# Streaming an MLP's first weights by rows instead of from re-laid column blocks

## The chip, the cores and the metric

The kernel runs on one core of one Trainium2 chip. The time is the device time of one execution in microseconds (us); a run list is quoted by its median. A profile is one execution of the kernel recorded by the hardware.

## The reference, cut to what matters

Two layers alternate twice: an attention layer (A) with recurrent memory over 64 segments of 32 tokens, and a Mixer layer (B) over the same 2048 tokens of width 640. The change touches B alone.

```python
def _B_ref(x, w1, w2, w3, w4):            # w1, w2: 640x640; w3: 640x1536; w4: 1536x640
    h = _gelu(_layernorm(x, axis=-1) @ w1)
    c = D // 4                            # 160 columns a group
    g0 = jnp.pad(h[:, :, 0*c:1*c], ((0,0),(1,0),(0,0)))[:, :S, :]     # one token later
    g1 = jnp.pad(h[:, :, 1*c:2*c], ((0,0),(0,1),(0,0)))[:, 1:, :]     # one earlier
    g2 = ...   # two later
    g3 = ...   # two earlier
    hs = jnp.concatenate([g0, g1, g2, g3], axis=-1) @ w2
    x1 = x + hs
    h2 = _gelu(_layernorm(x1, axis=-1) @ w3) @ w4
    return x1 + h2
...
x = x + A(layernorm(x)); x = x + B(layernorm(x))     # and both once more
```

## The kernel before

Both A layers run as two lanes, 40 columns of a matmul each, one segment per step; the second lane follows 5 steps behind. So there are 69 steps of about 50 us. Every two steps a chunk of Mixer (64 tokens of each lane, so 128 columns) runs among the attention: 35 chunks. A planner written in Python, before anything runs, places each operation on its engine. It takes what can start first by its own estimates, and among operations that could start nearly at the same time the one with the earlier `due`. The programs of the engines then wait for each other by semaphores.

Most of the weights stream from DRAM through a ring of 16 buffers in SBUF, on-chip memory (tile `wst`). Attention may hold 14 of them and Mixer 6. Attention's are issued by SyncE, Mixer's by GpSimd. Of the banks of PSUM, the memory that matmuls sum into, the kernel keeps two for the sums of `psy` and `y`, and shares six: class P (projections psq, psk, psv) may hold 4, class S (scores and the like: pss, pst, pso, psvt) 3, Mixer's class B 2.

```python
RING = 16; RING_A = 14; RING_B = 6
STEP = 48.0
W3 = (0.7, 0.04)        # due of w3's loads: from 0.7 of a step, every 0.04
PSUM_BANKS = {"y": 2, "x": 6}
PSUM_USES = {"y": ("y", 2), "P": ("x", 4), "S": ("x", 3), "B": ("x", 2)}
...
# Plan.place(): per engine e
lim = m + (LOOK if e == "PE" else 0.05)        # m: the earliest possible start
s, o = min((so for so in vals if so[0] <= lim), key=lambda so: (so[1].due, so[1].i))
```

w1's columns were taken in an order that puts each group's first 128 columns in one block and all the groups' remaining 4 x 32 in the fifth. The columns of w3 were taken in 12 blocks of 128. To make such a block one plain transfer, the kernel first copied w1, w3 and the last block of w2 within DRAM (`wbd`), in its first 25 us:

```python
def load_b(c, nm, n, due):
    b = ring("rb")
    k = {"w1": n, "w3": KC + n, "w2": KC + FC - 4 + n}.get(nm)
    ...
        src, rd = wbd[k], [B("wbd", k)]
    # nc.gpsimd.dma_start(out=T(b)[:, 0:Dm], in_=src)

def order_mixer_weights():
    for n in range(KC):             # five blocks of w1, gathered columns
        ...
    ...                             # one of w2
    for n in range(FC):             # twelve of w3
        def f3(op, n=n):
            o = wbd[KC + n].rearrange("p (kc n) -> p kc n", kc=KC)
            nc.gpsimd.dma_start(out=o, in_=B_w3.rearrange("(kc p) n -> p kc n", p=P)[:, :, P*n:P*n + P])
```

A column block completes 128 outputs by itself. Three of them share a PSUM bank, which goes to gelu while the next bank fills:

```python
for i, (a, e) in enumerate(((0, 3), (3, KC))):          # w1: banks of 3 and 2 blocks
    pz = ps("B", [P, 3, XB], f32, "psh")
    for n in range(a, e):
        due = D(0.15 + 0.04 * n)
        wb, wv = load_b(c, "w1", n, due)
        def fw(op, n=n, a=a, wv=wv, pz=pz):
            w, o = wv(), T(pz)
            for kc in range(KC):
                nc.tensor.matmul(out=o[:, n - a, :], lhsT=w[:, kc*P:(kc+1)*P],
                                 rhs=vT[:, kc, 4:XB + 4], start=(kc == 0), stop=(kc == KC - 1))
        add("PE", mm_us(128, k=KC), due, fw, r=(wb, vTk, B("vTl")), a=(pz,))
    ...
    gelu(pz, e - a, i, due, outs, (B("hTB", i),))
# w2: five blocks, the shift in time is an offset into hTB (W2OFF) -> bank pair hs
# w3: four banks of three blocks each, same loop; then w4 in 12 blocks -> bank pair y
```

gelu is: ScalarE square, VectorE scale and multiply, ScalarE tanh, VectorE (1 + tanh) times the sum, written into `outs`.

## Time and profile before

| Quantity | Before | From |
|---|---|---|
| time, median of 3 runs | 3567.71 us | times |
| PE busy in the whole span | 95% | page |
| PE busy, 1000 to 2000 us | 97.9% | stretches |
| PE time not used by matmuls, 400 to 3200 us | 124 us | matmul starts, as in the prediction |
| psk and psq waiting for their streams, 130 to 3440 us | 34 us | waits of PE |
| last chunk of Mixer alone, from the last psy to the last y matmul | 42.0 us | timeline |

In a page, "PE" is the matmul side of TensorE and "PEld" its weight loads. A line of a stretch gives its bounds and length, busy us (and count) of PE, PEld, DVE (VectorE), ACT (ScalarE) and POOL (GpSimd), then the granted clock, the DMA engines' busy share and GB/s. A line of the waits reads: engine, tile and line of the waiter, "<-", what it waited for, then us in total, times, longest. The page leaves numbers out of names: `in_B_w_dram` is any of w1 to w4. The lines themselves stand in the prediction.

### The profile page before, as it was taken

To read this page: it belongs to the slowest core of one execution; us is meant where nothing else is said; L and a number is where in the kernel's file an instruction comes from. 1 tells how busy PE (TensorE), PEld (TensorE's weight loads), DVE (VectorE), ACT (ScalarE), POOL (GpSimd) and SP (SyncE) were. 2 spreads that over 40 slices of the span, in tenths; PEclk is the share of its full clock that TensorE was granted. 3 is DMA by queue.
4 is the path that set the end of the run, shared out by engine and by line. 5 is a ranking of instruction groups with operands and counts; after the bars stand their busy time and mean duration, and the time that the engine had idled before them with its cause. 6 is when DMAs were issued, how large, how long until landed. Compare 5 with 4: busy or idle time off the path is not lost.

```text
span 3573.5 us, 194593 instructions
## 1 busy us (share of the span) xinstructions
PE 3398.9 (95%) x84703; PEld 3260.5 (91%) x84703; DVE 2384.2 (67%) x7085; ACT 1710.5 (48%) x3584; POOL 948.2 (27%) x1712
## 2 busy tenths in 40 slices
PE   5899999999999999999999999999999999999996
PEld 4788999999999999999999999999999999999885
DVE  2456667777676777776666777776767777776555
ACT  2344555554454555544455555454545555444432
POOL 3022222222222222222222222222222222222224
PEclk9999999999999999999999999999999999999898
DMA  9999999999999999999999999999999999999996
GB/s 342 310 314 312 305 302 304 310 308 308 309 307 313 314 308 304 316 300 308 306 308 311 311 301 305 308 319 308 309 311 310 311 306 313 309 304 316 310 313 207
DMA packets 735993, 1097.76 MB, mean 307 GB/s; under 512 B 97374, under 2 KB 693612, under 8 KB 735136
## 3 DMA queue, kind: packets, MB, share of 16 engines
q1 hardware_dynamic: 669504, 874.19, 74.6%
q0 software_dynamic: 65632, 211.12, 17.9%
q8 instruction: 662, 10.85, 1.3%
q14 instruction: 195, 1.60, 0.1%
HBM read 1079.68 MB, written 8.19 MB: 304 GB/s over the span
## 4 chain that ended last, share of the span: by engine, by line
PE 69%; DMA 19%; issue 9%; POOL 2%; DVE 1%; ACT 0%; POOLq 0%; SPq 0%; ACTq 0%; DVEq 0%
PE psy L669 14%; PE psq L530 12%; PE psv L571 11%; PE psk L530 11%; DMA wst<-in_A_Wk_dram 7%; DMA wst<-in_A_Wq_dram 5%; PE psvt L583 4%; DMA wst<-in_B_w_dram 4%; PE pss L602 3%; PE pso L650 3%; PE psh L993 3%; DMA wst<-in_A_Wv_dram 3%; PE pst L635 2%; PE y L1011 2%; POOL wst L465 1%
## 5 line engine op out<-in xcount | busy, mean ns | idle before, releaser
L530 PEld LDWEIGHTS <-wst 128*128 128x128 bf16 x13248 | 551.9, 100 | 75.1 <-DMA wst<-in_A_Wk_dram 41.3
L587 ACT COPY V<-psvt 80x768 bf16<-80x768 bf16 (+1 forms) x552 | 438.2, 794 | 327.7 <-PE psvt L583 326.2
L465 POOL DMA_DIRECT2D wst<-in_B_w_dram x560 | 303.6, 542 | 1005.2 <-PE psk L530 250.6
L656 DVE CAST oT<-pso 128x480 bf16<-128x480 f32 (+1 forms) x552 | 340.8, 617 | 341.7 <-PE pso L650 341.0
L465 POOL DMA_DIRECT2D wst<-wbd x630 | 339.6, 539 | 724.8 <-PE pss L602 229.5
L669 PE MATMUL psy<-oT,wo 128*128 128x80 bf16 (+1 forms) x10350 | 509.6, 199 | 11.2 <-DMA wo<-in_A_Wo_dram 5.1
L538 ACT CAST qT<-psq 128x480 bf16<-128x480 f32 (+1 forms) x552 | 292.3, 530 | 428.8 <-PE psq L530 427.5
L530 PE MATMUL psk<-hT,wk 128*128 128x80 bf16 (+1 forms) x9936 | 482.7, 199 | 7.9 <-ACT hT L707 4.2
L571 PE MATMUL psv<-hT,wv 128*128 128x80 bf16 (+1 forms) x9936 | 466.6, 199 | 6.5 <-DMA wv<-in_A_Wv_dram 4.3
L530 PE MATMUL psq<-hT,wq 128*128 128x80 bf16 (+1 forms) x9936 | 454.5, 199 | 9.8 <-DMA wq<-in_A_Wq_dram 8.7
L577 ACT CAST vTs<-psv 128x480 bf16<-128x480 f32 (+1 forms) x552 | 292.3, 529 | 337.2 <-PE psv L571 335.5
L669 PEld LDWEIGHTS <-wo 128*128 128x128 bf16 x10350 | 425.6, 100 | 21.3 <-issue 9.2
L530 PEld LDWEIGHTS <-wk 128*128 128x128 bf16 x9936 | 411.6, 99 | 21.9 <-issue 8.8
L571 PEld LDWEIGHTS <-wv 128*128 128x128 bf16 x9936 | 399.8, 100 | 18.7 <-DMA wv<-in_A_Wv_dram 5.7
L613 DVE CUSTOM_DVE_ANT_1 pss<-pss,mask 80x320 f32<-80x320 f32 (+1 forms) x512 | 245.4, 479 | 253.8 <-PE pss L602 252.3
L530 PEld LDWEIGHTS <-wq 128*128 128x128 bf16 x9936 | 395.5, 100 | 16.3 <-DMA wq<-in_A_Wq_dram 9.5
L530 PE MATMUL psk<-hT,wst 128*128 128x80 bf16 (+1 forms) x6624 | 359.0, 199 | 32.2 <-DMA wst<-in_A_Wk_dram 28.2
L571 PE MATMUL psv<-hT,wst 128*128 128x80 bf16 (+1 forms) x6624 | 368.0, 199 | 8.7 <-DMA wst<-in_A_Wv_dram 4.8
L625 DVE TENSOR_REDUCE sm<-pss 80x4 f32<-80x320 f32 (+1 forms) x552 | 252.7, 458 | 153.6 <-ACT pss L620 153.1
L669 PE MATMUL psy<-oT,wst 128*128 128x80 bf16 (+1 forms) x6210 | 353.0, 199 | 1.0 <-DMA wst<-in_A_Wo_dram 0.5
L530 PE MATMUL psq<-hT,wst 128*128 128x80 bf16 (+1 forms) x6624 | 333.2, 200 | 16.3 <-DMA wst<-in_A_Wq_dram 14.3
L546 DVE CAST kT<-psk 128x320 bf16<-128x320 f32 (+1 forms) x552 | 254.7, 461 | 136.9 <-PE psk L530 132.6
(119 smaller groups left out, 5768.8 us busy)
## 6 DMA issues: line engine op xcount, KB each, us to landing
wst<-in_A_Wk_dram SPq DMA_DIRECT2D x1104, 192.0 KB, 4.7
wst<-in_A_Wq_dram SPq DMA_DIRECT2D x1104, 192.0 KB, 4.9
wst<-in_A_Wv_dram SPq DMA_DIRECT2D x1104, 192.0 KB, 4.9
wst<-in_A_Wo_dram SPq DMA_DIRECT2D x1242, 160.0 KB, 4.4
wst<-wbd POOLq DMA_DIRECT2D x630, 160.0 KB, 5.1
wst<-in_B_w_dram POOLq DMA_DIRECT2D x560, 160.0 KB, 4.9
wk<-in_A_Wk_dram SPq DMA_DIRECT2D x8, 576.0 KB, 7.3
wq<-in_A_Wq_dram SPq DMA_DIRECT2D x8, 576.0 KB, 7.5
```

The lines of the kernel that those rows point to most:

```text
L465: return (nc.sync if B_SP else nc.gpsimd).dma_start(out=T(b)[:, 0:Dm], in_=src)
L530: nc.tensor.matmul(out=o[:, c, 0:N], lhsT=w[:, c * P:(c + 1) * P], rhs=h[:, kc, c0:c0 + N], start=pq.begin(), stop=True, skip_group_check= ...
L538: nc.scalar.copy(out=q[:, :, 0:N], in_=T(pq)[:, :, 0:N])
L546: nc.vector.tensor_copy(out=k4[:, :, 0::3, 0:N], in_=p4[:, :, 0::2, 0:N])
L571: nc.tensor.matmul(out=o[:, c, 0:N], lhsT=w[:, c * P:(c + 1) * P], rhs=h[:, kc, c0:c0 + N], start=pv.begin(), stop=True, skip_group_check= ...
L577: nc.scalar.copy(out=vs[:, :, 0:N], in_=T(pv)[:, :, 0:N])
L583: nc.tensor.transpose(out=T(pt)[0:N, c, :], in_=vs[:, c, 0:N], identity=ident[:, :])
L587: nc.scalar.copy(out=V_[0:N, :, 0:Dh], in_=T(pt)[0:N].rearrange("n c f -> n (c f)").rearrange("n (i e) -> n i e", i=HG))
L613: nc.vector.tensor_tensor_reduce(out=o, in0=o, in1=maskt.unsqueeze(1).to_broadcast([N, HG, N]), scale=-scale, scalar=3.0e38, op0=ALU.add, ...
L625: nc.vector.reduce_sum(out=sm_[0:N, 4:4 + HG], in_=o, axis=AX.X)
L656: nc.vector.tensor_copy(out=o_[:, :, 0:N], in_=T(pso)[:, :, 0:N])
L669: nc.tensor.matmul(out=T(psy[j])[:, m - m0, c0:c0 + N], lhsT=w[:, m * P:(m + 1) * P], rhs=o_[:, c, 0:N], start=psy[j].begin(), stop=True, ...
```

## The change

The intent is to do without the copies. Rows of w1 and w3 are contiguous in DRAM as they lie. A block of 128 rows holds a part of the sum of every output, so all the outputs must stay open in PSUM until the last block: five column groups over two banks for w1, six over two banks for each half of w3. Without the gathered column order, w1's outputs lie in their plain order, and each 160-column group must be written shifted by gelu: nine pieces where there were six. Mixer's ring share goes from 6 to 5 and w3's loads are spaced wider.

```diff
-RING_B = 6
+RING_B = 5
-W3 = (0.7, 0.04)
+W3 = (0.75, 0.055)
+W1 = (0.15, 0.04)
...
-    wbd = dram.tile([KC + FC + 1, P, Dm], bf16, name="wbd")
...
     def load_b(c, nm, n, due):
         b = ring("rb")
-        k = {"w1": n, "w3": KC + n, "w2": KC + FC - 4 + n}.get(nm)
+        wd = Dm
+        if nm == "w1":
+            src = B_w1[P * n:P * n + P, :]
+        elif nm == "w3":
+            wd = F // 2
+            src = B_w3[P * (n % KC):P * (n % KC) + P, wd * (n // KC):wd * (n // KC) + wd]
...
-    def order_mixer_weights():        (whole function and its call)
...
-        for i, (a, e) in enumerate(((0, 3), (3, KC))):
-            pz = ps("B", [P, 3, XB], f32, "psh")
-            for n in range(a, e):
...
+        pz = [ps("B", [P, 3, XB], f32, "psh") for _ in range(2)]
+        for kc in range(KC):
+            due = D(W1[0] + W1[1] * kc)
+            wb, wv = load_b(c, "w1", kc, due)
+
+            def fw(op, kc=kc, wv=wv, pz=pz):
+                w = wv()
+                for n in range(KC):
+                    nc.tensor.matmul(out=T(pz[n // 3])[:, n % 3, :], lhsT=w[:, P * n:P * n + P],
+                                     rhs=vT[:, kc, 4:XB + 4], start=pz[n // 3].begin(), stop=True,
+                                     skip_group_check=True)
+            add("PE", mm_us(128, k=KC), due, fw, r=(wb, vTk, B("vTl")), a=tuple(pz))
...
+        outs = [], []
+        for n in range(KC):
+            p0 = 0
+            while p0 < P:
+                gi = (P * n + p0) // QD
+                p1 = min(P, QD * (gi + 1) - P * n, p0 + 32 if p0 % 64 else (P if p0 == 0 else p0 + 64))
+                o2 = 2 * (4 - W2OFF[gi])
+                outs[n // 3].append((p0, p1, n % 3, n % 3 + 1, hv[p0:p1, n:n + 1, o2:o2 + XB]))
+                p0 = p1
+        for i in range(2):
+            gelu(pz[i], 3 - i, i, due, outs[i], (B("hTB", i),))
...
-                off = W2OFF[n] if n < 4 else 0
-                lhsT = hTB[:, n, off:off + TOK, :].rearrange("p w l -> p (w l)")
+                lhsT = hTB[:, n, 0:TOK, :].rearrange("p w l -> p (w l)")
...
-        for i in range(4):             (w3, three column blocks to a bank)
...
+        for hf in range(2):
+            pz = [ps("B", [P, 3, XB], f32, "psh2") for _ in range(2)]
+            for kc in range(KC):
+                due = D(W3[0] + W3[1] * (KC * hf + kc))
+                wb, wv = load_b(c, "w3", KC * hf + kc, due)
+                ...                    (six matmuls a row block, over both banks)
+            for i in range(2):
+                a = 6 * hf + 3 * i
+                gelu(pz[i], 3, i, due, [(0, P, 0, 3, h2T[:, a:a + 3, :])], (B("h2T", 2 * hf + i),))
```

More of the change, by code (lines that the diff above doesn't have):

```diff
@@ L455, in load_b @@
         b = ring("rb")
-        k = {"w1": n, "w3": KC + n, "w2": KC + FC - 4 + n}.get(nm)
-        if nm == "w4":
-            src, rd = w4_v[:, n, :], []
-        elif nm == "w2" and n < 4:
-            src, rd = B_w2[QD * n:QD * n + P, :], []
+        wd = Dm
[4 more added lines that the diff above has]
+            src = B_w3[P * (n % KC):P * (n % KC) + P, wd * (n // KC):wd * (n // KC) + wd]
+        elif nm == "w4":
+            src = w4_v[:, n, :]
         else:
-            src, rd = wbd[k], [B("wbd", k)]
+            src = B_w2[P * n:P * n + P, :]
         def fn(op):
-            return (nc.sync if B_SP else nc.gpsimd).dma_start(out=T(b)[:, 0:Dm], in_=src)
-        add("SP" if B_SP else "POOL", SP_US if B_SP else POOL_US, due, fn, r=rd, w=(b,), dma=P * Dm * 2, queue="wb")
-        return b, lambda: T(b)[:, 0:Dm]
-    def order_mixer_weights():
-        for n in range(KC):
-            def f(op, n=n):
-                o = wbd[n].rearrange("p (kc n) -> p kc n", kc=KC)
-                w1 = B_w1.rearrange("(kc p) n -> p kc n", p=P)
-                if n < 4:
-                    nc.gpsimd.dma_start(out=o, in_=w1[:, :, QD * n:QD * n + P])
-                    return
-                for gi in range(4):
-                    nc.gpsimd.dma_start(out=o[:, :, 32 * gi:32 * gi + 32], in_=w1[:, :, QD * gi + P:QD * gi + QD])
-            add("POOL", 0.9 if n < 4 else 4.0, 20 + n, f, w=(B("wbd", n),), dma=P * Dm * 2)
-        def f2(op):
-            for gi in range(4):
-                nc.gpsimd.dma_start(out=wbd[KC + FC][32 * gi:32 * gi + 32, :], in_=B_w2[QD * gi + P:QD * gi + QD, :])
-        add("POOL", 4.0, 26, f2, w=(B("wbd", KC + FC),), dma=P * Dm * 2)
-        for n in range(FC):
-            def f3(op, n=n):
-                o = wbd[KC + n].rearrange("p (kc n) -> p kc n", kc=KC)
-                nc.gpsimd.dma_start(out=o, in_=B_w3.rearrange("(kc p) n -> p kc n", p=P)[:, :, P * n:P * n + P])
-            add("POOL", 0.9, 30 + n, f3, w=(B("wbd", KC + n),), dma=P * Dm * 2)
+            return (nc.sync if B_SP else nc.gpsimd).dma_start(out=T(b)[:, 0:wd], in_=src)
+        add("SP" if B_SP else "POOL", SP_US if B_SP else POOL_US, due, fn, w=(b,), dma=P * wd * 2, queue="wb")
+        return b, lambda: T(b)[:, 0:wd]
     def lanes(t):
@@ L929, in chunk @@
         add("POOL", 0.4, D(0.05), fhh, w=(B("hTB", 0), B("hTB", 1)))
-        for i, (a, e) in enumerate(((0, 3), (3, KC))):
-            pz = ps("B", [P, 3, XB], f32, "psh")
-            for n in range(a, e):
-                due = D(0.15 + 0.04 * n)
-                wb, wv = load_b(c, "w1", n, due)
-                def fw(op, n=n, a=a, wv=wv, pz=pz):
-                    w, o = wv(), T(pz)
-                    for kc in range(KC):
-                        nc.tensor.matmul(out=o[:, n - a, :], lhsT=w[:, kc * P:(kc + 1) * P],
-                                         rhs=vT[:, kc, 4:XB + 4], start=(kc == 0), stop=(kc == KC - 1))
-                add("PE", mm_us(128, k=KC), due, fw, r=(wb, vTk, B("vTl")), a=(pz,))
-            hv = hTB[:].rearrange("p k w l -> p k (w l)")
-            if e <= 4:
-                outs = [(0, P, 0, e - a, hv[:, a:e, 8:8 + XB])]
-            else:
-                outs = [(0, P, 0, 4 - a, hv[:, a:4, 8:8 + XB])]
-                for gi in range(4):
-                    o2 = 2 * (4 - W2OFF[gi])
-                    outs.append((32 * gi, 32 * gi + 32, 4 - a, 5 - a, hv[32 * gi:32 * gi + 32, 4:5, o2:o2 + XB]))
-            gelu(pz, e - a, i, due, outs, (B("hTB", i),))
@@ new lines, in chunk @@
+        hv = hTB[:].rearrange("p k w l -> p k (w l)")
+        outs = [], []
[9 more added lines that the diff above has]
+            gelu(pz[i], 3 - i, i, due, outs[i], (B("hTB", i),))
@@ L982, in chunk, with fw @@
         add("ACT", act_us(KC * XB), D(0.55), fe3, r=(ps3,), w=(vTk,))
-        for i in range(4):
-            a, e = 3 * i, 3 * i + 3
-            pz = ps("B", [P, 3, XB], f32, "psh2")
-            for n in range(a, e):
-                due = D(W3[0] + W3[1] * n)
-                wb, wv = load_b(c, "w3", n, due)
-                def fw(op, n=n, a=a, wv=wv, pz=pz):
-                    w, o = wv(), T(pz)
-                    for kc in range(KC):
-                        nc.tensor.matmul(out=o[:, n - a, :], lhsT=w[:, kc * P:(kc + 1) * P],
-                                         rhs=vT[:, kc, 0:XB], start=(kc == 0), stop=(kc == KC - 1))
-                add("PE", mm_us(128, k=KC), due, fw, r=(wb, vTk), a=(pz,))
-            gelu(pz, 3, i % 2, due, [(0, P, 0, 3, h2T[:, a:e, :])], (B("h2T", i),))
+        for hf in range(2):
[3 more added lines that the diff above has]
+                wb, wv = load_b(c, "w3", KC * hf + kc, due)
+                def fw(op, kc=kc, wv=wv, pz=pz):
+                    w = wv()
+                    for n in range(6):
+                        nc.tensor.matmul(out=T(pz[n // 3])[:, n % 3, :], lhsT=w[:, P * n:P * n + P], rhs=vT[:, kc, 0:XB],
+                                         start=pz[n // 3].begin(), stop=True, skip_group_check=True)
+                add("PE", mm_us(128, k=6), due, fw, r=(wb, vTk), a=tuple(pz))
+            for i in range(2):
+                a = 6 * hf + 3 * i
+                gelu(pz[i], 3, i, due, [(0, P, 0, 3, h2T[:, a:a + 3, :])], (B("h2T", 2 * hf + i),))
     def chunk_end(c):
@@ L1077, in start @@
             add("ACT", act_us(KC * SEG), -90 + s, f5, r=(p1,), w=(B("hT", s, "x0"),))
-        order_mixer_weights()
     start()
```

## The prediction

> **What bounds the kernel now.** I read four views in this order: the page's busy shares and slices, the busy time per stretch, the list of who waited for whom, and PE's timeline of the last 50 us.
>
> The page first (span; busy us, share and count of each engine; then the 40 slices):
>
> ```profile
> span 3573.5 us, 194593 instructions
> PE 3398.9 (95%) x84703; PEld 3260.5 (91%) x84703; DVE 2384.2 (67%) x7085; ACT 1710.5 (48%) x3584; POOL 948.2 (27%) x1712
> PE   5899999999999999999999999999999999999996
> ...
> DMA  9999999999999999999999999999999999999996
> ```
>
> PE and the DMA engines are both above nine tenths in every slice but the first two and the last. So there are three stages: a start, a long even middle, and a tail. The busy time per stretch (columns: stretch, its length, PE, PEld, DVE, ACT, POOL busy us with counts, granted clock, DMA share, GB/s) says what limits each:
>
> ```profile
> 10.00:20.00 10.00, 5.13 (x105) 4.33 (x105) 2.25 (x9) 2.11 (x8) 10.00 (x16) 1.00 1.07 376
> ...
> 80.00:100.00 20.00, 13.88 (x275) 11.11 (x273) 3.76 (x15) 3.94 (x9) 0.00 (x0) 1.00 1.07 366
> ...
> 1000.00:2000.00 1000.00, 978.97 (x24325) 954.67 (x24323) 703.82 (x2030) 504.47 (x1031) 263.59 (x474) 1.00 0.94 309
> ...
> 3500.00:3574.00 74.00, 42.10 (x709) 32.70 (x709) 33.66 (x94) 18.28 (x41) 34.60 (x63) 0.77 0.54 175
> ```
>
> In the start, until about 110 us, the DMA share stands at 1.07 and 366 to 376 GB/s while PE is busy half to two thirds: the start is bound by transfers. In the middle PE is 98% busy, and DMA runs at 0.94 and 309 GB/s, which is 83% of the 371 GB/s it showed it can do: the middle is bound by PE, with DMA close behind. The tail is a chain of latencies: the last Mixer chunk has no attention beside it.
>
> How much slack is left in the middle? From the trace's matmul starts between 400 and 3200 us I took the distance of each of 67,992 from the next, which sums to 2800 us, and subtracted the columns of each at 2.4 per ns plus 2.5 ns[...], which sums to 2676 us. Only 124 us are left to win there by any means. The waits of PE (middle only, 130 to 3440 us: waiter, what it waited for, us in total, times, longest) name the largest parts:
>
> ```profile
> PE psk L530 <- DMA wst<-in_A_Wk_dram: 22.7, 40, 1.4
> PE y L1011 <- DMA wst<-in_B_w_dram: 13.3, 25, 1.5
> PE psq L530 <- DMA wst<-in_A_Wq_dram: 11.2, 19, 1.4
> ```
>
> No line of the Mixer's w1 or w3 loads stands among the large ones: the loads of the copies (wst<-wbd) cost PE 0.8 us in the whole run. What PE waits for there is attention's streams and w4.
>
> **What the Trainium skill says.** (1) "DMA: Bandwidth & Descriptors", section "Issuing engines are not separate DMA queues": transfers issued from any engine run on the same 16 DMA engines. The trace agrees: while GpSimd issues the copies at 10 to 20 us, the total stays at 376 GB/s, no higher than the 371 to 372 later without them, so their bytes displace weights. (2) The same page, "Why small descriptors are slow (HBM only)": a 256-byte descriptor pays 27% bus overhead unless consecutive ones are put in one packet. The copies are cut into 256-byte and 64-byte pieces, so they could be dear, but the trace's packet records show them as packets of 4096, 2048 and 2560 bytes, and 4096 bytes took 178 ns (23 GB/s for an engine) against 73 ns for the 1536 bytes of attention's rows (21 GB/s): not dear here. (3) "TensorE: Matmul & The Clock Gate", "Back-to-back issue gap": 128 columns take N/2.4 + 2.5 = 56 ns. The trace agrees: ten psh matmuls at 3516.06 us span 0.72 us, and less the 0.22 us of the last that is 9 distances of 56 ns. (4) "PSUM — Partial Sum Buffer", "The four PSUM rules": a start flag clears the written marks of the whole bank, so several sums open in one bank need the flag on the first matmul alone. That is what the new loops do; so summing by rows over two banks needs no extra instruction. No run so far shows a cost of it.
>
> **The change, part by part.**
>
> *Copies removed.* The page says that 8.19 MB are written to DRAM: out 2.62, x2d 2.62, and 18 blocks of 163,840 bytes, 2.95 MB, the copies. Packets: 512 of 4096 B at 178 ns, 256 of 2048 B at 90, 158 of 2560 B at 107, 22 of 3840 B at 215: 91 + 23 + 17 + 5 = 136 us of one engine, 8.5 us of all 16. They are issued from 4.9 to 24 us, in the stage bound by transfers, so nearly all 8.5 us come off the path: **-8.5 us**. GpSimd also loses 24 issues (21 us busy), which hold back nothing before 115 us, where the first Mixer chunk starts.
>
> *Streaming w1 and w3 by rows.* w1: 5 blocks of 160 KB as before. w3: 10 blocks of 128x768 (192 KB) in place of 12 of 160 KB: the same 1.97 MB per chunk. So 32 loads per chunk in place of 34, 1120 in place of 1190. A contiguous block went as 5120-byte packets at 243 ns; half rows of w3 must go as 1536 bytes at 73 ns: 47.5 against 47.7 ns per KB, no difference. 70 issues fewer at 0.54 us each is 38 us of GpSimd, which is 27% busy: **0 us**.
>
> *Matmuls.* By the two builds' instruction orders both have 84,703, of the same shapes in the same numbers (2975 for w1 and w3). The order of attention's transfers on SyncE is the same line for line. Only the place of Mixer's matmuls among attention's moves: **0 us** of PE.
>
> *Shifts made by gelu.* The last gelu step of w1 was one 128x384 (543 ns), one 128x128 (276) and four 32x128 (282): 1.95 us per chunk. Now it is nine pieces of 128 columns at about 280: 2.5 us. 35 chunks x 0.57 = 20 us of VectorE, 67% busy: hidden in the middle.
>
> *Two banks held together.* w1 and each half of w3 now keep both Mixer banks from the first row to the end of the gelus; the two halves of w3 can't overlap. In the middle attention fills PE meanwhile. In the tail it shows:
>
> ```profile
> 3537.80 2.83 PE L939 MATMUL psh<-vT,wst 128*128 128x128 bf16 x25 [0.78 <-ACT vT L914]
> 3542.53 2.83 PE L961 MATMUL hs<-wst,hTB 128*128 128x320 bf16 x10 [1.90 <-issue]
> ...
> 3550.86 5.17 PE L993 MATMUL psh<-vT,wst 128*128 128x128 bf16 x60 [0.83 <-ACT vT L981]
> 3556.19 1.98 PE L1011 MATMUL y<-wst,h2T 128*128 128x320 bf16 x10 [0.16 <-DVE h2T L781]
> ```
>
> The first gelu of w1 began 1.1 us before psh x25 was over (3539.65, by the timeline of all engines); now it waits for all 25, and has 0.6 us more VectorE: about +1.5 us. For w3, a gelu takes 3.5 us (3552.65 to 3556.1); a half is 30 x 56 ns = 1.7 us, its two gelus end about 4.5 us later, and only then the other half starts: 2 x (1.7 + 4.5) = 12.4 us to the last h2T, after which three pairs of y matmuls take 0.8: y ends 13.2 us after the start of w3 against 11.7 now (3550.86 to 3562.58): **+3 us** for both.
>
> *Ring.* Mixer may hold 5 of the 16 ring buffers in place of 6, so attention gets one more at the busiest times, and w3's loads are due every 0.055 of a 48 us step (2.6 us) in place of 1.9: smoother. This should take some of the 34 us that psk and psq wait for their streams in the middle and could add to y's 13. I choose **-6 us**, a judgement.
>
> Sum: 3567.7 - 8.5 + 3 - 6 = 3556; I take **3555**.
>
> **Rivals.** *PSUM becomes the wait.* With both Mixer banks held, attention has 4 of the 6 shared banks for longer (about 1.6 steps in place of 1 in each pair of steps). For it: the scores and projections may ask for 7. Against: PE's unused time is no higher while hs or y hold two banks than elsewhere; binned over the chunk, it peaks at the step ends instead. If it happened, I'd expect 0.5 us per step, 35 us: 3590. *DMA is the true bound of the middle.* Then fewer buffers for Mixer and smoother loads would lift the whole 124 us by a good part: 3567.7 - 8.5 - 50 = 3510. Against it: 309 of 371 GB/s, and PE's waits on DMA there sum to 50 us. *The start is hidden anyway*: if PE had to wait for something else at 100 us, the 8.5 us vanish and the time stays at 3565. Against: PE's longest waits up to 130 us, after the first data, name wq, wo and wv arriving.
>
> **Range and chances.** The three runs before span 8 us. Start and tail together are worth -5, certain to about 5; the middle may go 25 us either way as the order on PE moves. 3530 to 3574 should hold it 8 times in 10. 2% is 71 us, more than half of all that PE leaves unused in the middle, so faster by 2% has 0.03, slower by 2% 0.03, and the same 0.94.
>
> **What would show it.** HBM written falls to 5.24 MB, read by 2.95 MB. The stretch in which the DMA share is above 1.05 ends some 8 us earlier. PE's busy share from 1000 to 2000 us stays within 97 to 99%. The waits of psk and psq on their streams fall, those of y may rise. In the tail psh for w3 comes as two groups of 30 with a gap of some 4 us. I'm wrong if the middle moves by over 25 us: then bank waits (psk or pss waiting for ACT or DVE) or stream waits must have changed by that much.

## More of the kernel before

In the compiled program an instruction waits only for the bank that it was given.

## The result and the profile after

The changed kernel took 3571.62 us (median of 4 runs, 3565.49 to 3574.00) and the kernel before 3565.85 us (4 runs, 3561.39 to 3569.81). The ratio is 1.0014, with a 95% interval of 0.9996 to 1.0032: the same. A ratio here is always the mean time of one kernel's fast runs over that of the other's of the same rounds, so it is not quite the ratio of the medians. The time is inside the predicted range and 17 us above the predicted value. The profiled executions were 3575.23 us (before) and 3571.54 us (changed).

The page of the changed kernel, its span, busy times and bytes:

```profile
span 3569.8 us, 194617 instructions
...
PE 3394.6 (95%) x84703; PEld 3260.5 (91%) x84703; DVE 2383.4 (67%) x7190; ACT 1709.6 (48%) x3584; POOL 895.0 (25%) x1618
...
HBM read 1076.73 MB, written 5.24 MB: 303 GB/s over the span
```

The same 84,703 matmuls take the same time. VectorE has 105 instructions more and isn't busier. GpSimd has 94 fewer. The written bytes have fallen from 8.19 to 5.24 MB, as foreseen.

The busy time by stretch of the changed kernel, for the stretches that the prediction showed:

```profile
10.00:20.00 10.00, 4.75 (x97) 3.93 (x98) 2.25 (x9) 1.59 (x6) 1.22 (x3) 1.00 1.05 366
...
80.00:100.00 20.00, 12.94 (x273) 10.90 (x271) 1.40 (x5) 2.94 (x7) 0.00 (x0) 1.00 1.05 356
...
1000.00:2000.00 1000.00, 975.14 (x24225) 951.64 (x24222) 704.24 (x2062) 504.45 (x1029) 255.16 (x458) 1.00 0.94 308
...
3500.00:3574.00 74.00, 39.64 (x599) 30.23 (x595) 31.22 (x87) 16.14 (x36) 33.13 (x60) 0.76 0.47 153
```

The start is as full of transfers as it was, the middle runs at 97.5% of PE in place of 97.9%, and fewer matmuls are left for the last 74 us. So the gain of the start was not lost in the middle by much. What PE waited for there has changed its names, though. The waits of PE between 130 and 3440 us in the changed kernel:

```profile
PE pst L615 <- DVE Pm L607: 17.1, 28, 0.6
PE y L995 <- DMA wst<-in_B_w_dram: 14.4, 27, 1.4
PE psk L510 <- issue: 10.9, 18, 1.4
...
PE psk L510 <- DMA wst<-in_A_Wk_dram: 5.8, 12, 1.3
...
PE psq L510 <- DMA wst<-in_A_Wq_dram: 1.8, 4, 0.7
```

The streams' waits of psk and psq fell from 33.9 us to 7.6, while the waits of both that the profile puts down to nothing ("issue") rose from 4.0 us to 17.2. At the top stands a wait that the kernel before doesn't have among its large ones: the transposes of the probabilities (pst) wait for VectorE 28 times, 0.6 us each. Time that matmuls leave unused in the middle, measured as in the prediction, is 123.3 us after 124.3: the new waits took nearly all that the old ones gave.

PE's timeline of the last 50 us in the changed kernel (start, length, what, and in brackets the idle time before it and its releaser):

```profile
3520.91 0.43 PE L995 MATMUL y<-wst,h2T 128*128 128x320 bf16 x2 [2.04 <-DMA wst<-in_B_w_dram]
...
3538.08 2.83 PE L918 MATMUL psh<-vT,wst 128*128 128x128 bf16 x25 [0.78 <-ACT vT L894]
3543.35 3.23 PE L944 MATMUL hs<-wst,hTB 128*128 128x320 bf16 x10 [2.44 <-issue]
...
3552.08 5.70 PE L975 MATMUL psh<-vT,wst 128*128 128x128 bf16 x60 [0.84 <-ACT vT L964]
...
3558.28 1.80 PE L995 MATMUL y<-wst,h2T 128*128 128x320 bf16 x12 [0.51 <-DVE h2T L761]
...
3561.32 1.80 PE L995 MATMUL y<-wst,h2T 128*128 128x320 bf16 x12 [1.24 <-DVE h2T L761]
```

Against the prediction's fence: from the start of w1 to the start of w3 it is 14.0 us, after 13.06. From the start of w3 to the end of the last y matmul it is 11.04 us (3552.08 to 3563.12), after 11.72. And the y of the chunk before stood 2.04 us for w4's load. The whole tail went from 42.0 to 46.8 us. The clock clouds the lengths: the granted clock was half until 3553.7 us in the kernel before and from 3549.9 to 3556.7 us in the changed one, and there the psh matmuls of w3 stand 107 ns apart, not the 56 ns that the prediction reckoned with.

### The profile page after: what moved, and what is told of

Its sections match the earlier page's. It is cut to its first block, busy times and chain, and to the rows that moved or that the text cites. A ratio compares the mean times of both kernels' runs of the same rounds, so it can differ in the third digit from the quotient of the medians.

```text
span 3569.8 us, 194617 instructions
## 1 busy us (share of the span) xinstructions
PE 3394.6 (95%) x84703; PEld 3260.5 (91%) x84703; DVE 2383.4 (67%) x7190; ACT 1709.6 (48%) x3584; POOL 895.0 (25%) x1618
## 3 DMA queue, kind: packets, MB, share of 16 engines
HBM read 1076.73 MB, written 5.24 MB: 303 GB/s over the span
## 4 chain that ended last, share of the span: by engine, by line
PE 78%; DMA 12%; DVE 4%; issue 4%; POOL 1%; ACT 0%; SPq 0%; DVEq 0%; POOLq 0%; ACTq 0%
PE psy L649 15%; PE psq L510 14%; PE psv L551 13%; PE psk L510 13%; PE psvt L563 4%; PE pss L582 4%; DMA wst<-in_B_w_dram 4%; PE pso L630 4%; PE psh L975 3%; DMA wst<-in_A_Wk_dram 3%; PE y L995 2%; PE pst L615 2%; DMA wst<-in_A_Wq_dram 2%; DMA wst<-in_A_Wv_dram 2%; PE hs L944 1%
## 5 line engine op out<-in xcount | busy, mean ns | idle before, releaser
L468 POOL DMA_DIRECT2D wst<-in_B_w_dram x1120 | 606.1, 542 | 1744.1 <-PE pss L582 285.1
L510 PE MATMUL psq<-hT,wq 128*128 128x80 bf16 (+1 forms) x9936 | 474.6, 199 | 14.0 <-DMA wq<-in_A_Wq_dram 8.9
L551 PE MATMUL psv<-hT,wv 128*128 128x80 bf16 (+1 forms) x9936 | 453.2, 199 | 4.0 <-DMA wv<-in_A_Wv_dram 2.5
L510 PEld LDWEIGHTS <-wq 128*128 128x128 bf16 x9936 | 407.7, 99 | 29.8 <-DMA wq<-in_A_Wq_dram 9.8
L551 PEld LDWEIGHTS <-wv 128*128 128x128 bf16 x9936 | 390.8, 99 | 14.4 <-DMA wv<-in_A_Wv_dram 3.9
L620 ACT COPY PT<-pst 80x320 bf16<-80x320 bf16 (+1 forms) x552 | 221.8, 402 | 296.7 <-PE pst L615 293.1
L551 PE MATMUL psv<-hT,wst 128*128 128x80 bf16 (+1 forms) x6624 | 350.0, 199 | 10.7 <-DMA wst<-in_A_Wv_dram 7.9
L605 DVE TENSOR_REDUCE sm<-pss 80x4 f32<-80x320 f32 (+1 forms) x552 | 252.9, 458 | 154.5 <-ACT pss L600 153.0
L649 PE MATMUL psy<-oT,wst 128*128 128x80 bf16 (+1 forms) x6210 | 338.4, 199 | 1.2 <-DMA wst<-in_A_Wo_dram 0.8
L600 ACT ACTIVATE pss<-pss,sm 80x320 f32<-80x320 f32 (+1 forms) x552 | 261.6, 474 | 141.1 <-DVE sm L593 141.1
```

The costliest lines, as they stand in the source:

```text
L468: return (nc.sync if B_SP else nc.gpsimd).dma_start(out=T(b)[:, 0:wd], in_=src)
L510: nc.tensor.matmul(out=o[:, c, 0:N], lhsT=w[:, c * P:(c + 1) * P], rhs=h[:, kc, c0:c0 + N], start=pq.begin(), stop=True, skip_group_check= ...
L551: nc.tensor.matmul(out=o[:, c, 0:N], lhsT=w[:, c * P:(c + 1) * P], rhs=h[:, kc, c0:c0 + N], start=pv.begin(), stop=True, skip_group_check= ...
L600: nc.scalar.activation(out=o, in_=o, func=ACT.Exp, bias=sm_[0:N, 0:1], scale=-1.0)
L605: nc.vector.reduce_sum(out=sm_[0:N, 4:4 + HG], in_=o, axis=AX.X)
L620: nc.scalar.copy(out=Pt[0:N, :, 0:N], in_=T(pst)[0:N, :, 0:N])
```

## The experiments

Twelve runs were made (e9 is the changed kernel again). Runs of one call shared the chip and the runs of the kernel before. Those medians differ by 10 us between chips (3569.82 on the first, 3578.45 on the second, 3575.56 on the third), so only the ratios compare. "Unused" is PE time not used by matmuls from 400 to 3200 us. "Streams" is psk and psq waiting for theirs from 130 to 3440 us, and "y on w4" the same for y; all three are of one profiled execution. The last column names a wait of PE for another engine that comes 25 times or more.

| Kernel | Chip | Median us | Ratio to before [95%] | Unused | Streams | y on w4 | Once-a-chunk wait of PE |
|---|---|---|---|---|---|---|---|
| before | – | 3565.85 | 1 | 124.3 | 33.9 | 13.3 | none |
| changed | – | 3571.62 | 1.0014 [0.9996, 1.0032] | 123.3 | 7.6 | 14.4 | pst on Pm, 17.1 |
| e1, copies back | 1st | 3585.68 | 1.0040 [1.0012, 1.0067] | 130.2 | 12.4 | 21.0 | pst on Pm, 17.4 |
| e2, ring of 6 | 1st | 3566.91 | 0.9993 [0.9968, 1.0018] | 116.5 | 16.0 | 1.7 | psq on V, 20.3 |
| e3, one piece | 1st | 3578.66 | 1.0021 [0.9995, 1.0047] | 120.9 | 6.1 | 18.6 | pst on Pm, 17.5 |
| e4, w3 by rows only | 1st | 3554.97 | 0.9958 [0.9932, 0.9983] | 100.7 | 10.2 | 21.1 | pso on PT, 7.1 |
| e5, w1 bank by bank | 2nd | 3588.97 | 1.0034 [1.0010, 1.0059] | 135.6 | 6.0 | 27.7 | psq on V, 5.2 |
| e6, gelu due later | 2nd | 3578.99 | 1.0010 [0.9987, 1.0034] | 122.2 | 9.6 | 17.7 | pst on Pm, 17.4 |
| e7, w3 spaced only | 2nd | 3578.07 | 1.0011 [0.9984, 1.0038] | 116.8 | 8.6 | 22.2 | pso on PT, 6.9 |
| e8, w1 by rows only | 2nd | 3581.85 | 1.0016 [0.9993, 1.0039] | 124.7 | 28.2 | 9.7 | psq on V, 19.7 |
| e9, changed again | 3rd | 3573.29 | 0.9997 [0.9981, 1.0012] | 119.5 | 11.4 | 15.0 | pst on Pm, 17.5 |
| e10, w3 by rows, ring of 6 | 3rd | 3561.60 | 0.9953 [0.9936, 0.9970] | 103.5 | 29.9 | 2.3 | none |
| e11, bank by bank, ring of 6 | 3rd | 3552.14 | 0.9932 [0.9917, 0.9948] | 99.0 | 15.3 | 0.7 | none |
| e12, w1 in strips, ring of 6 | 3rd | 3588.54 | 1.0031 [1.0015, 1.0046] | 129.8 | 15.4 | 6.0 | psq on hTB, 8.3 |

The theory had three parts. The copies gave their 8 us in the start. The tail took some 5 back. In the middle, letting both of w1's banks end together makes a wait, which eats what spacing and ring had won. The rivals: the nine pieces of the last gelu step fill VectorE; Mixer's five ring buffers starve y and others; the two halves of w3 hold the banks too long; or it is all the noise of a schedule.

### e1: the copies put back

```diff
+    wbd = dram.tile([KC + FC + 1, P, Dm], bf16, name="wbd")
+    def order_mixer_weights(): ...        # as in the kernel before; nothing reads wbd
+        order_mixer_weights()             # at the end of start()
```

> The changed kernel with the 24 copies into DRAM issued again at the start (2.95 MB, read by nobody); the order of instructions on VectorE and SyncE is that of the changed kernel, on PE nearly so. If the start is bound by transfers, as the prediction has it, the time rises by 8.5 us over the changed kernel (about 3580) and the stretch with a DMA share above 1.05 lasts 8 us longer. Rival (the start is hidden, or the lead is lost later anyway): no change, 3571.

The ratio was 1.0040 and the interval excludes 1. Against the changed kernel's 1.0014 and 0.9997 (e9) this is 0.26 to 0.43%, so 9 to 15 us. The first 100 us of the kernel before:

```profile
0.00:100.00 100.00, 56.02 (x1092) 45.23 (x1093) 21.07 (x90) 19.62 (x47) 29.34 (x55) 1.00 1.00 344
```

The same stretch of the changed kernel:

```profile
0.00:100.00 100.00, 60.21 (x1190) 48.86 (x1191) 21.62 (x92) 19.97 (x49) 10.25 (x30) 1.00 0.99 338
```

And of e1, with the copies back:

```profile
0.00:100.00 100.00, 56.75 (x1102) 45.67 (x1102) 21.02 (x90) 19.66 (x47) 28.89 (x54) 1.00 1.00 344
```

The DMA share is 0.99 to 1.00 in all three, so what bounds this stretch is the same. In slices of 5 us from 60 us on it stays at 1.05 or more up to 105 us before, 95 changed and 105 here, as the prediction said that it would. Without copies PE is 98 matmuls further by 100 us; with them back it falls to 1102. The fifth attention step ended at 298.2 us before, 292.9 changed and 300.5 here. The copies' cost is shown, and so is that nothing else in the start took it back. The profiled executions of e1 and of the changed kernel end 20 us apart, though, and only some 7 of these lie in the start; the rest came later, where no copies run, and isn't explained.

### e2: six ring buffers for Mixer in the changed kernel

```diff
-RING_B = 5
+RING_B = 6
```

> The changed kernel with 6 ring buffers for Mixer in place of 5. If the smaller ring is what starves w4 in the tail (y of the last chunk but one waited 4.4 us on its loads against 1.6 before), those waits fall below 2 us and about 3 us come off the tail. If the smaller ring is also what took the stream waits of psk and psq from 34 us to 8 us in the middle, they come back to about 30 us. Net: between -3 and +15 us against the changed kernel. Rival (the stream waits fell because w3's loads are spaced wider): they stay near 8 us.

The ratio was 0.9993. The two large waits of PE in it, 130 to 3440 us:

```profile
PE psq L510 <- ACT V L567: 20.3, 29, 0.7
...
PE psk L510 <- DMA wst<-in_A_Wk_dram: 8.4, 15, 1.3
```

y's wait for w4 falls from 14.4 to 1.7 us, and the streams' waits rise from 7.6 to 16.0, not to the 30 that was expected if the ring alone had lowered them: the sixth buffer moves a wait between the two users of the ring. The tail missed its forecast: y still waited 3.4 us there, and it took 45.7 us, 1.1 less and not 3. The first line says more. The projection psq does not read V. V is the copy that ScalarE makes from the bank of psvt, so by elimination psq is waiting for that bank. So the once-a-chunk wait can show at pst or at psq, depending on the order, and in this form it is a PSUM wait, the first rival of the prediction.

### e3: gelu's last step of w1 in one piece per bank (wrong result)

```diff
-            gelu(pz[i], 3 - i, i, due, outs[i], (B("hTB", i),))
+            gelu(pz[i], 3 - i, i, due, [(0, P, 0, 3 - i, hv[:, 3 * i:3 * i + 3 - i, 8:8 + XB])], (B("hTB", i),), (6, 3)[i])
```

The last argument keeps the planner's duration at nine pieces, so PE's order is the same. The shifts in time are missing. (The comparison with the reference passed all the same, so it does not test these shifts.)

> The changed kernel with each gelu of w1 written in one piece, without the shifts in time (wrong result on purpose), the planner's durations and so every engine's order kept. It takes 7 of 9 small VectorE writes away per chunk. If the nine pieces are what makes pst wait for Pm (17 us in the middle, 28 times), that wait falls under 3 us and the time by 10 to 17 us. Rival (the wait is the gelu's first VectorE pair falling between a score group's exp and its sum): the wait stays at 15 to 18 us and the time falls by less than 3 us.

The ratio was 1.0021, and pst still waited 17.5 us, 28 times. The number of pieces isn't the cause, and it costs nothing that shows.

### e4: the kernel before with w3 alone by rows

```diff
 (against the kernel before)
-RING_B = 6
+RING_B = 5
-W3 = (0.7, 0.04)
+W3 = (0.75, 0.055)
+  w3's loads, loop and two halves as in the changed kernel; its 12 copies dropped
   w1, w2, their copies and the shifts as before
```

> The kernel before with w3 alone streamed by rows over two banks, with the changed ring (5) and spacing of w3; w1, w2 and the shifts stay as before, and 6 of 18 copied blocks stay. If w1's two banks ending together are what makes pst wait for Pm, that wait is under 5 us here while the stream waits of psk and psq are low as in the changed kernel (under 15 us): time 3555 to 3562. Rival (w3's halves or the ring cost the time): no better than the changed kernel, 3568 to 3575.

The ratio was 0.9958, faster than both by more than its interval. Its waits of PE for w4 and for ScalarE's PT:

```profile
PE y L1010 <- DMA wst<-in_B_w_dram: 21.1, 34, 1.9
PE pso L648 <- ACT PT L638: 7.1, 31, 0.3
```

There is no 17 us wait of pst or psq, though w3's halves hold both banks just as in the changed kernel. Its unused time is 100.7 us. Therefore w3 by rows helps, and what harms comes with w1.

### e5: w1 by rows, but one bank after the other

```diff
+W1B = 0.015
+        rows = []
         for kc in range(KC):
+            rows.append(load_b(c, "w1", kc, D(W1[0] + W1[1] * kc)))
+        for i in range(2):
+            for kc in range(KC):
+                due = D(W1[0] + W1[1]*kc) if i == 0 else D(W1[0] + W1[1]*KC + W1B*(kc + 1))
                 ...
-                for n in range(KC):
+                    for n in range(3 * i, min(KC, 3 * i + 3)):
...
-            gelu(pz[i], 3 - i, i, due, outs[i], (B("hTB", i),))
+            gelu(pz[i], 3 - i, i, dues[i], outs[i], (B("hTB", i),))
```

> The changed kernel, with w1's five row blocks kept until all have landed in use: first all matmuls into bank 0, then all into bank 1, so that the first gelu starts before the second bank is full (same loads, matmuls and results). If w1's two banks ending together are what costs PE its once-a-chunk wait (pst for Pm 17 us here, psq for V's copy 20 us with 6 ring buffers), no wait of 25 times or more stands in the middle any more and the time falls by about 15 us against the changed kernel, to some 3555. Rival (Mixer's rows in general, or order at large): such a wait stays or another takes its place, and the time stays within 6 us of the changed kernel.

The ratio was 1.0034, a miss: some 3555 us was expected. The once-a-chunk wait fell to 5.2 us (still 29 times), but two others came, which the waits of PE show:

```profile
PE y L1002 <- DMA wst<-in_B_w_dram: 27.7, 44, 1.4
...
PE psh L982 <- DMA wst<-in_B_w_dram: 9.2, 17, 1.3
```

All five row blocks of w1 stay in the ring until the second bank has passed over them, and five are all that Mixer has. So w4 (y) and w3 (psh L982) were issued late. That is a statement about the ring of 5, and e11 tests it.

### e6: w1's gelu made due later

```diff
-            gelu(pz[i], 3 - i, i, due, outs[i], (B("hTB", i),))
+            gelu(pz[i], 3 - i, i, due + 0.08 * STEP, outs[i], (B("hTB", i),))
```

> The changed kernel with only the due time of w1's two gelus set 3.8 us later, so that attention's work of the same time goes first on VectorE and ScalarE. If the order on VectorE is the cause of pst's wait for Pm, it falls from 17 us under 5 us; the time by up to 15 us. Rival: the wait moves to hs or to another pair, time within 6 us of the changed kernel.

The ratio was 1.0010, and pst waited 17.4 us, 28 times, as before the edit. The planner takes what can start first; `due` decides only within 0.05 us. So the edit did not move gelu behind the softmax, and the run tells nothing about what that would be worth.

Where the wait of pst comes from is shown by the timeline of all engines of the changed kernel, at one chunk:

```profile
1470.04 0.49 ACT L600 ACTIVATE pss<-pss,sm 80x320 f32<-80x320 f32 x1
...
1471.00 0.35 DVE L751 TENSOR_SCALAR gl<-gl 128x384 f32<-128x384 f32 x1
...
1471.45 0.56 DVE L752 TENSOR_TENSOR gl<-gl,psh 128x384 f32<-128x384 f32 x1
...
1471.93 0.48 DVE L605 TENSOR_REDUCE sm<-pss 80x4 f32<-80x320 f32 x1
...
1472.72 0.49 DVE L607 TENSOR_TENSOR Pm<-pss,sm 80x320 bf16<-80x320 f32 x1
...
1473.26 0.34 PE L615 MATMUL pst<-ident,Pm 80*80 80x80 bf16 x4 [0.62 <-DVE Pm L607]
```

The exponentials of a score group (L600) are ready at 1470.53. VectorE's sum over them (L605) starts at 1471.93, because VectorE first finishes the Pm of the group before and then does two steps of the gelu of w1's first bank (L751, L752; 384 columns): 0.9 us of delay. The normalized Pm is therefore ready after PE's other work is used up, and pst waits 0.62 us. All 28 of these waits have the same steps before them. The steps of the second bank's gelu are not among them.

A gelu between the steps of a softmax isn't enough, though. The kernel before has the same two steps there; one chunk of its timeline of all engines:

```profile
971.29 0.48 ACT L620 ACTIVATE pss<-pss,sm 80x320 f32<-80x320 f32 x1
...
971.98 0.55 DVE L772 TENSOR_TENSOR gl<-gl,psh 128x384 f32<-128x384 f32 x1
...
972.45 0.48 DVE L625 TENSOR_REDUCE sm<-pss 80x4 f32<-80x320 f32 x1
...
973.92 0.32 PE L635 MATMUL pst<-ident,Pm 80*80 80x80 bf16 x4
```

The sum starts 0.7 us after its exponentials, in 29 of the 35 chunks, and pst follows without idle time of PE. In the changed kernel it is 1.4 us. So it is the moment that differs: what VectorE has just done, and what PE has left to do. No run changes that alone.

### e7: only spacing and ring, on the kernel before

```diff
 (against the kernel before)
-RING_B = 6
+RING_B = 5
-W3 = (0.7, 0.04)
+W3 = (0.75, 0.045)
```

> The kernel before, all copies kept and w3 by columns, with the changed ring (5) and w3's loads spread over the changed span (0.75 to 1.25 of a step in place of 0.70 to 1.14). If the spacing and the ring, and not the rows, are what took the stream waits of psk and psq from 34 to under 15 us in the run with w3 alone by rows, they are under 15 us here too and the time is 3552 to 3560. Rival (the rows, or both banks): they stay above 25 us, time 3564 to 3572.

The ratio was 1.0011: nothing won. The streams' waits fell from 33.9 to 8.6 us, as in the changed kernel, so that part of the prediction's sixth step is due to spacing and ring. But y's wait for w4 rose to 22.2 us and waits that the profile puts down to nothing ("issue") came:

```profile
PE psq L530 <- issue: 14.5, 19, 2.4
```

Set against e4, which differs by w3's rows (ten blocks due every 0.055 where these are twelve every 0.045, the same stretch of time) and by the absence of their 12 copies, it is 0.53% (19 us; the two ran on different chips). The 12 copies are 5.7 us of that by the prediction's own working (8.5 us x 12/18), and at 100 us e4 is 5.9 us ahead of the kernel before. What makes up the other 13 us stays open. One thing is easily missed in e7: its unused time is 7.5 us lower than before, and its tail 5 us longer (47.0 us). The profiles of the changed kernel and of e9 differ by 3.8 us in unused time, so 7.5 is only twice that. Still, spacing and ring may have won in the middle what they lost in the tail.

### e8: only w1 by rows

```diff
 (against the changed kernel)
-RING_B = 5
+RING_B = 6
-W3 = (0.75, 0.055)
+W3 = (0.7, 0.04)
+  w3's twelve copies, loads and loop as in the kernel before
```

> The complement of the run with w3 alone: the kernel before with w1 by rows and the shifts made by gelu, w3 by columns from copies (12 of 18 blocks copied), ring 6 and w3's old spacing. Theory (w1's new loop costs the middle some 15 us, w3's change gains some 20): the stream waits of psk and psq stay above 25 us, a once-a-chunk wait on VectorE or ScalarE of some 15 us is there as well, the time is 3575 to 3590. Rival: it is as fast as the kernel before or faster.

The ratio was 1.0016. psq waited 19.7 us for V, 29 times, as in e2, and the streams' waits are back at 28.2 us, as with the old spacing. So w1 by rows, by itself, shows no gain from its six missing copies, and its mark is the once-a-chunk wait.

### e9: the changed kernel again

> The changed kernel itself again, so that it stands beside the others on one chip in the same rounds. So far it is 1.0014 of the kernel before with an interval from 0.9996 to 1.0032. If its gains (start 8 us, stream waits 26 us) and its losses (w1's once-a-chunk wait 17 us, y and the tail some 5 us) do cancel, it stays between 0.998 and 1.003.

There is no edit. The ratio was 0.9997 [0.9981, 1.0012] on another chip, and its waits have the same names and sizes. Between the two measurements, 1.0014 and 0.9997, lie 6 us; both agree with no change at all.

### e10: w3 by rows with six ring buffers

```diff
 (against e4)
-RING_B = 5
+RING_B = 6
```

> The fastest so far (w3 alone by rows, w1 and w2 as before) with 6 ring buffers for Mixer in place of 5. Waits of y for w4 in the middle, 21 us with 5, should fall under 10 us, those of psk and psq rise from 10 us to some 16 us, and the tail shorten by 2 us: 0.991 to 0.996 of the kernel before. Rival (the gain of w3 alone was chance of the order): above 0.998.

The ratio was 0.9953, as e4's, and far from the rival's 0.998: the gain of w3 by rows came twice, on two chips. Its waits of PE:

```profile
PE psk L528 <- DMA wst<-in_A_Wk_dram: 15.8, 28, 1.5
...
PE y L1010 <- DMA wst<-in_B_w_dram: 2.3, 7, 0.7
```

The streams wait 29.9 us again, almost as in the kernel before, y hardly at all, and the time is that of e4, where it was the other way around. So the total under one name of a wait says little of the time: here one wait filled in for another.

### e11: one bank after the other, with six ring buffers

```diff
 (against e5)
-RING_B = 5
+RING_B = 6
```

> The run with w1 bank by bank, with 6 ring buffers in place of 5. If that run was slow because w1's five blocks held every ring buffer of Mixer (w4 waits 28 us, w3 waits 9 us), both fall under 10 us here, the once-a-chunk waits stay under 8 us, and the time is 0.993 to 0.998 of the kernel before. Rival: it stays above 1.001.

The ratio was 0.9932 [0.9917, 0.9948]: 3552.14 us against 3575.56, and the fastest of all. It beats both kernels. Its waits of PE:

```profile
PE psk L511 <- DMA wst<-in_A_Wk_dram: 9.1, 18, 1.4
...
PE y L1002 <- DMA wst<-in_B_w_dram: 0.7, 2, 0.4
```

y's wait for w4 is gone, and psh no longer waits for w3; both were the ring's, as e5 suggested. There is no once-a-chunk wait of any size. The unused time is 99.0 us. Against e2, which differs only in whether w1's banks end together (and so in how long its blocks stay in the ring), it is 0.61% (22 us), and the two intervals are apart, though the two ran on different chips, each against the kernel before on its own.

### e12: w1 in column strips, with six ring buffers

```diff
 (against e2)
+  w1 as ten blocks: 5 x [128, 384] for the first bank, then 5 x [128, 256] for the second,
+  each due 0.5 * W1[1] after the one before
```

> The changed kernel with w1 as ten blocks, five of 128x384 for the first bank and then five of 128x256 for the second, and 6 ring buffers: each block is freed after its own bank, the banks end one after the other. Theory: no once-a-chunk wait over 8 us, w4 waits under 10 us, 0.992 to 0.997 of the kernel before. Rival (five more transfers per chunk cost more than they free): 1.000 or more.

The ratio was 1.0031, slower than the kernel before. The strips also end the banks one after the other, but ten smaller blocks come too late, which the waits of PE show:

```profile
PE psh L921 <- DMA wst<-in_B_w_dram: 10.5, 15, 3.7
```

The matmuls of w1 themselves (psh L921) wait up to 3.7 us for their blocks, w2's (hs) 5.6 us in total. A ring buffer holds 768 columns, and the strips fill half of it or a third. So staggering the banks paid with whole blocks (e11) and not with strips (e12); that the number of blocks is the reason fits the waits, but no run separates it from their due times.

## Why the prediction was right, and where it was wrong

**In sum.** 3555 was predicted, -12 us, in a range of 3530 to 3574; 3571.62 came. The range held it and the class is right. That is partly luck: a gain that the prediction put at 0 (w3 by rows) and a loss that it didn't see (w1's banks) nearly cancel. The parts, though, did not add up as written: -8 in the start, -1 in the middle and +5 in the tail give -4 in the profiled executions (3575.23 to 3571.54), and between -1 and +5 in the two timed comparisons.

**Copies, -8.5 us: right.** By matmul starts the changed kernel reaches the same work some 7 us earlier between 68 and 161 us (6.4 to 8.8), and e1 undid it. The rival that the start is hidden anyway is refuted. Two slips in the working don't matter: the 22 packets of 3840 bytes and 30 of those of 2560 are in the changed kernel too, so they aren't copies and the sum is 8.0 us; and 376 GB/s during the copies is a little above the 371 to 372 later, not "no higher".

**Streaming by rows, "0 us": mis-sized for w3.** The step counted bytes, packets and issues. Bytes and issues are as it said; the half rows went as packets of 4608 and 3072 bytes in place of 1536, at much the same time per byte (48.5 ns per 1000 bytes against 47.5). But w3 by rows alone is worth -0.42% (e4) and -0.47% (e10), 15 to 17 us, of which the missing 12 copies are 5.7 us. The step had no term for when the blocks come and leave, and I haven't found the mechanism of the rest. It lies in the middle: the unused time is 100.7 and 103.5 us where it was 124.3. It is not the lower streams' waits, as e10 has almost those of the kernel before. That it is not spacing and ring of 5 alone is shown by e7. The new spacing with column blocks and six buffers was not run.

**Matmuls, 0 us: right.** There are 84,703 in both, 3398.9 and 3394.6 us busy. The section that the prediction names for 56 ns gives it for a matmul by itself, and about 81 ns for 128 columns in a stream with weight loads. Here the median distance of the psh matmuls, each with a weight load of its own, is 56 ns from 400 to 3200 us in the kernel before.

**Shifts made by gelu, hidden: right about the pieces** (e3), **but a part was missing.** The prediction saw the gelus of w1 end together only in the tail. "In the middle attention fills PE meanwhile" is the step that failed there: pst waits 17 us for Pm, or psq 20 us for V. In the first form the steps of the first bank's gelu stand before the softmax's on VectorE; in e2 ScalarE does that gelu's tanh and then a softmax's exponentials before the copy of V, 29 times alike. All six kernels whose w1 banks end together under the row order (changed, e1, e2, e3, e6, e8; and e9, the same kernel) have it at 17 to 20 us, and those whose banks end one after the other have at most 8.3. With six ring buffers the one edit is worth 22 us (e2 against e11). That ending the banks together brings the wait is shown by this. Why the gelu then comes at a moment when PE has nothing else to do is argued from the timelines only, as the kernel before has a gelu between a softmax's steps at no cost.

**Two banks held, +3 us in the tail: near, by wrong parts.** It is +4.8 us. The w1 part was put at +1.5 and is +0.9. The w3 part was put at +1.5 (13.2 against 11.7) and is -0.7 (11.04): the two halves of w3 went as one unbroken group of 60 matmuls (5.70 us), where two groups with a gap of 4 us had been foreseen. "The two halves of w3 can't overlap" failed: it is a limit in the planner's own times only. The second half's last matmul started at 3557.56 us, before the first half's gelus had begun to write h2T (3557.68), so it was in other banks. In its place the y of the last chunk but one waited 4.4 us for w4 in place of 1.6, with the delay passed on to the tail: +4 in the stretch from its last psy. Spacing shows here more than the ring: with 6 buffers and the old spacing (e8) y waited some 2 us and the tail was 43.6 us; with 6 and the new spacing (e2, e10) y still waited 3.4 and 4.2 us and the tail was 45.7. The stretches of half clock lie differently in each tail, which blurs these lengths by a us or two.

**PSUM as a rival: argued away too soon.** It was to show as bank waits of 35 us, and it shows as 20 us in e2 and e8, in a form where psq waits for the bank that ScalarE's copy of V leaves. The argument against it (unused time no higher while hs or y hold two banks) looked at w2 and w4, whose banks don't go to a gelu.

**Ring and spacing, -6 us: the mechanism right, the gain absent.** The streams' waits fell by 26 us. The unused time fell by 1 (by 4.8 in e9). The step that failed is "this should take some of the 34 us ... -6 us": it took a wait's total for time that could be won, and had no term for the once-a-chunk wait of 17 us that took its place. e7 and e10 show the two sides of it: waits cut to a quarter without a gain in the whole time, and a gain with the waits almost as they were.

**What stays open.** Why w3's row blocks beat spaced column blocks by another 9 to 13 us; and how much of each ratio is the luck of one schedule, as any edit moves PE's order everywhere. Runs of one kernel on one chip spread by 17 to 35 us (kernel before: 3552.42 to 3587.05 on the first), and the intervals are 0.15 to 0.27% to either side, so differences under some 0.25% are not told apart here.

## What to carry to other kernels

When a change makes results become ready together or at another moment, look at which engine takes them up and whose steps it stands between, in every stage and not only in the last; ending them one after the other was worth 22 us here, with a ring buffer more for Mixer (with the ring of 5 it lost). Don't price a change by the waits that it removes while PE stays 97% busy; compare PE's unused time, and expect that another wait may fill in. Do a combined change part by part: here one part (w3 by rows) was worth 15 us, and another (w1 with both banks ending together) took it away.

## What the Trainium skill lacked or had wrong

- "Runtime: NRT & Kernel Launch", section "Instruction fetch mechanics", says that crossing an instruction block of 16 KiB is mostly hidden. In the kernel before, from 400 to 3200 us, 152 gaps of PE are over 0.2 us (86 us in all), and 76 of them (49 us) end 0.9 to 1.75 us after an instruction packet of 16,384 bytes landed, where chance would give 24. All the kernels show 25 to 49 us of such gaps. It is an association in time; no run here took the fetches away.
- "TensorE: Matmul & The Clock Gate", section "HAM oscillation — how this bites in real kernels", gives as the rule that PE's idle gaps longer than about 3.4 us bring the clock down. Here the granted clock went to half for windows of 3.4 or 6.8 us, four times between 3300 and 3400 us of the kernel before, with no start-to-start distance of matmuls over 1.45 us in the 8 us before a drop. (The page's next section does tell of another kernel in which frequent short idle gaps had this effect.) The stretch of the kernel before in which one lane of attention is left, with the clock third from the end:

```profile
3300.00:3400.00 100.00, 93.85 (x2481) 82.50 (x2478) 55.81 (x204) 40.92 (x104) 25.77 (x48) 0.90 0.96 315
```

  PE was busy 93.85 of 100 us at a mean clock of 0.90. Over the whole span the mean granted clock was 0.986 to 0.992 in the runs of e1, e2, e4 and e11.
- No page that I found says how a wait for a PSUM bank is named in a list of waits: as a wait for an engine whose result the waiting instruction never reads (e2: psq on ScalarE's V, 20.3 us).
